# Fixing the engine order of the first batch, and the place of the weight conversions, in a three-stage attention, gated and spatial-gating kernel

## The chip, the cores and the metric

One core of one Trainium2 chip. The metric is device time in microseconds (us) of one execution; a kernel's time is the median of its runs. The kernel before took 771.68 us, the median of three runs (771.37 to 773.01).

## What is computed

Three blocks one after the other, for a batch of 8 sequences of 576 tokens with 512 channels, in fp32. The first two matter here:

```
kv  = einsum('bhsd,bhse->bhde', k, v)            # 8 heads of 64
o   = einsum('bhsd,bhde->bhse', q, kv)
x   = o / sqrt(mean(o*o, -1) + 1e-6) * g_norm    # heads joined: 512 channels

gate = sigmoid(causal 5-tap convolution of x along the tokens with conv_w)
y    = (gate * (x @ w_val)) @ w_out

...  # third block: y @ w_in, gelu, norm, a matmul over the tokens, @ w_out2, + y
```

The weights `w_val`, `conv_w`, `w_out`, `w_in` and `w_out2` reach the kernel as 64-bit floats, so each is read as pairs of 32-bit words and converted on the chip into a high part (fp32r, the format of the matmul) and a low part (the remainder). The products are formed as high*high + low*high + high*low.

## The kernel before, in words

**Tiling.** 512 channels are four groups m = 0 to 3 of 128. A batch has 512 main tokens (four tiles of 128) and 64 rest tokens (tile t = 4); the rest tokens of four batches are collected and multiplied together after batches 3 and 7. `x` is kept transposed: channels on partitions, tokens along the row. Every product with a weight (`gemm3`, L165, issued at L171) is 12 matmuls of 128 x 512.

**One batch.** `load_kv` and `load_q` (L192, L201) load; K, V and Q have one buffer each, so the next batch's load waits until the batch before has been read. `kv` (L205) forms the 64 x 64 products (80 matmuls, L220), `kv_out` copies them into a block-diagonal tile. `o(t)` (L234) gives one token tile (8 matmuls, L239) and queues three pieces: `norm` (square on ScalarE, sum on VectorE, scale and power -0.5 on GpSimd, L246 to L249), `scale` (VectorE, L252) and `transpose` (four on TensorE, L263; ScalarE copies into `x32`, L265, and into the high part, L268; VectorE forms the low part, L269). `conv(m)` (L283) is one ScalarE and four VectorE instructions (L285, L287) and a sigmoid. `Moe.val(m)` (L302) multiplies with `w_val` and queues `gated` (times the gate on VectorE, L312; high part on ScalarE; low part on GpSimd for m = 0 and 2, else on VectorE, L314). `Moe.out(m)` (L318) multiplies with `w_out`; all four m of the gated product have to be there first.

**Conversion of a weight** (`wide_parts`, L107, and `split`, L125). One piece is 128 columns of the weight, 128 x 512 elements on the chip for `w_val` and `w_out` (four pieces each, L560), 128 x 256 for `w_in` (16 pieces). A piece takes, in the form without GpSimd, an `Abs` on ScalarE (L113), L114 to L117 and L122 on VectorE, a copy on ScalarE (L151), a subtraction on GpSimd (L152) and an addition on VectorE (L153). With `on_pool` the product of L122 goes to ScalarE and GpSimd instead (L119, L120) and the addition to GpSimd. Half of the pieces of `w_val` and `w_out` have `on_pool` (L565). The raw words of `w_val` and `w_out` share one tile (`wiu` at that time), piece by piece; the pieces share two work areas (`wiv` at that time), so a third piece waits for the first. `w_in` later takes those two tiles over.

**What sets the order.** The program is written in slots: `later(n, fn, rank)` puts work n slots ahead, `tick` runs what is due. Beyond that the program is traced with a planner (L782) which, from a model of the time line, picks the order of instructions on each engine and may move an instruction ahead of others that stand before it in the program if its inputs are there. Each engine then runs its list strictly in order; SyncE's list holds every DMA issue. In the trace the conversion of `w_in`, which stands in the loop of batches 2 to 5 (L645 to L649), begins while batch 0 is still being prepared.

**The start before.** L565 to L611: the first two pieces of `w_val`, K and V, Q, the other two pieces and the small constants are loaded, two pieces are converted, then `kv` of batch 0, the `o` of batch 0 mixed with the loads of `w_out` and with `kv` of batch 1 (L592 to L600), then the other two pieces; the four `conv` and the four pieces of `w_out` are queued (L607 to L609), and the loop over the batches begins with `val` of batch 0 (L624).

Of the kernel before, what the change touches and what calls it, by code (L numbers as in the profile page):

```python
# [33 lines left out]
EXP_MAX = 1.875 * 2.0 ** -96  # L34

# [24 lines left out]
def body(ctx, tc, qT, k, v, gcol, w_val, conv_w, w_out, w_in, g_ln, w_sgT, b_sg, w_out2, out, out_r):  # L60
# [46 lines left out]
    def wide_parts(raw, t, on_pool):  # L107

        hi, lo = raw[:, :, 1], raw[:, :, 0]
        m, b, s = t[:, 0], t[:, 1].bitcast(I32), t[:, 2].bitcast(I32)
        act(m, hi.bitcast(F32), AF.Abs, scale=2.0 ** -112)  # L113
        ts(m, m, EXP_MAX, None, op0=ALU.min)  # L114
        ts(s, hi, -0x80000000, None, op0=ALU.bitwise_and)
        stt(b, m.bitcast(I32), 3, s, op0=ALU.logical_shift_left, op1=ALU.bitwise_or)
        ts(s, b, -0x800000, None, op0=ALU.bitwise_and)  # L117
# [5 lines left out]
        return f32(b), m  # L123

    def split(src, h, l, on_pool=False, raw=None, tmp=None, k=None):  # L125
# [8 lines left out]
        def start():  # L134
# [9 lines left out]
        def work():  # L144
# [5 lines left out]
            a, c = wide_parts(r.rearrange("p (n t) -> p n t", t=2), sb("cv", [3, n]) if tmp is None else tmp, on_pool)  # L150
# [4 lines left out]
        return start, work  # L155
# [25 lines left out]
    act(sb("st", [3, 8], bufs=3)[:, 0], mhalf, AF.Sigmoid)  # L181
# [5 lines left out]
    class Attention:  # L187
# [46 lines left out]
        def o(self, t, wait=3):  # L234
# [6 lines left out]
            st = sb("st", [3, 8], bufs=3)  # L241
# [3 lines left out]
            def norm():  # L245
                act(xo[:n], po[:n], AF.Square)  # L246
                nc.vector.tensor_reduce(st[:n, 0], x3, axis=AX.X, op=ALU.add)
                nc.gpsimd.tensor_scalar(st[:n, 1], st[:n, 0], 1.0 / DH, 1e-6, op0=ALU.mult, op1=ALU.add)
# [5 lines left out]

            later(0, norm, 0)
# [3 lines left out]
        def transpose(self, t, xo):  # L259
# [5 lines left out]
            act(x32[:, :, HALO + o:HALO + o + n], pt, AF.Identity, scale=gcol_s)  # L265
            if t < 4:
                xh, xl = self.xh[:, :, o:o + n], self.xl[:, :, o:o + n]
                act(xh, pt, AF.Identity, scale=gcol_s)  # L268
                stt(xl, pt, gcol_s, f32(xh), op0=ALU.mult, op1=ALU.subtract)  # L269
# [26 lines left out]
    class Moe:  # L296
# [5 lines left out]
        def val(self, m):  # L302
# [8 lines left out]
            def gated():  # L311
                tt(z, ps, self.g[:, m, :n], op=ALU.mult)  # L312
                act(zh, z, AF.Copy)
                (nc.gpsimd.tensor_tensor if m in (0, 2) else tt)(zl, z, f32(zh), op=ALU.subtract)  # L314

            later(0, gated, 0)

# [220 lines left out]

    def background(pieces, every, first=1, per=1):
# [20 lines left out]
    def first_weight(w, src, on_pool):  # L560
        return [split(src[:, m * P:(m + 1) * P], w[:, 0, :, m * P:(m + 1) * P], w[:, 1, :, m * P:(m + 1) * P],
                      on_pool[m], first[0][:, m], first[1][:, m % 2], k=NK)
                for m in range(NK)]

    wv_pieces, wo_pieces = first_weight(wv, w_val, (1, 0, 1, 0)), first_weight(wo, w_out, (0, 1, 1, 0))  # L565
    atts = [Attention(0)]
    wv_pieces[0][0]()
    wv_pieces[1][0]()
    atts[0].load_kv()
    atts[0].load_q()  # L570
    wv_pieces[2][0]()
    wv_pieces[3][0]()
    dma(gcol_s, gcol)
    dma(gln_s, g_ln)
    if conv_w.dtype == F32:
        dma(cw, conv_w)
    else:
        raw = sb("raw", [WC * 2], I32, bufs=2)[:, :2 * NK * KC]
        dma(raw, conv_w.bitcast(I32))
        a, c = wide_parts(raw.rearrange("p (n t) -> p n t", t=2), sb("cv", [3, NK * KC]), False)  # L580
        tt(cw, a, c, op=ALU.add)


    att = atts[0]
    wv_pieces[0][1]()
    wv_pieces[1][1]()
    att.kv(0)
    att.kv(1)
    tick()
    atts.append(Attention(1))  # L590
    atts[1].load_kv()
    for t in range(5):  # L592
        att.o(t, 2)
        tick()
        if t < 2:
            wo_pieces[t][0]()
        if t == 2:
            atts[1].kv(0)
            atts[1].kv(1)
            atts[1].load_q()  # L600
    tick()
    tick()
    wv_pieces[2][1]()
    wv_pieces[3][1]()
    wo_pieces[2][0]()
    wo_pieces[3][0]()
    for m in range(NK):  # L607
        later(m // 2, lambda m=m: att.conv(m), -1)
        later(m, wo_pieces[m][1], 3)  # L609
# [3 lines left out]
    for b in range(B):  # L613
        moe = Moe(atts[b].xh, atts[b].xl, gate, y_main[b])
# [8 lines left out]
        for s in range(8):  # L623
            if s < 4:  # L624
                moe.val(s)
            else:
                moe.out(s - 4)
            if b == 0 and s < 2:
                nxt.o(s)
# [15 lines left out]
            if b >= 2 and s % 2 and wi_n < len(wi):  # L645
                later(0, wi[wi_n][1], 3)
# [15 lines left out]
            tick()  # L662
        if b % RG == RG - 1:
# [124 lines left out]
```

## Time and profile before

| what | value |
|---|---|
| median of three runs | 771.68 us |
| the profiled execution | 771.06 us, of which the profile's span is 769.3 us |
| granted TensorE clock, mean over the span | 0.975 of 2.4 GHz |
| busy over the span: TensorE, VectorE, ScalarE, GpSimd | 94%, 77%, 46%, 23% |
| instructions | 11598 |

The profile has the busy time of each engine, the span in 40 slices, the chain of work that ended last, groups of instructions with what they waited for, and the DMA issues. A time line gives the start, the time taken and the count of like instructions that follow one another; the text in brackets is idle time of the engine in front of it and what ended it. PE is TensorE, DVE VectorE, ACT ScalarE, POOL GpSimd. A duration of a VectorE instruction overlaps the next one's by some 0.08 us when the two do not depend on each other.

### The profile page before, as it was taken

To read this page: it belongs to the slowest core of one execution; us is meant where nothing else is said; L and a number is where in the kernel's file an instruction comes from. 1 tells how busy PE (TensorE), PEld (TensorE's weight loads), DVE (VectorE), ACT (ScalarE), POOL (GpSimd) and SP (SyncE) were. 2 spreads that over 40 slices of the span, in tenths; PEclk is the share of its full clock that TensorE was granted. 3 is DMA by queue.
4 is the path that set the end of the run, shared out by engine and by line. 5 is a ranking of instruction groups with operands and counts; after the bars stand their busy time and mean duration, and the time that the engine had idled before them with its cause. 6 is when DMAs were issued, how large, how long until landed. Compare 5 with 4: busy or idle time off the path is not lost.

```text
span 769.3 us, 11598 instructions
## 1 busy us (share of the span) xinstructions
PE 724.7 (94%) x4400; PEld 621.9 (81%) x4400; DVE 590.2 (77%) x1118; ACT 350.0 (46%) x662; POOL 176.1 (23%) x186
## 2 busy tenths in 40 slices
PE   6529999999799999998999999999999999999997
PEld 6418778787787888887988988889899889898896
DVE  4979997988975968978977687776876867867662
ACT  3454755656535557456442343433432523434320
POOL 3763472635340725121000000010000000100000
PEclk8769999999999999999999999999999999999999
DMA  9852536355334310343212022121321221221203
GB/s 304 267 182 75 166 117 205 105 177 191 104 104 153 115 55 14 114 153 113 84 56 101 31 75 84 55 67 44 117 93 51 69 97 42 69 68 42 96 1 110
DMA packets 56199, 80.13 MB, mean 104 GB/s; under 512 B 3664, under 2 KB 29264, under 8 KB 55120
## 3 DMA queue, kind: packets, MB, share of 16 engines
q1 hardware_dynamic: 56144, 79.40, 31.1%
q8 instruction: 34, 0.56, 0.3%
q14 instruction: 21, 0.17, 0.1%
HBM read 60.51 MB, written 18.87 MB: 103 GB/s over the span
## 4 chain that ended last, share of the span: by engine, by line
PE 82%; DVE 7%; DMA 5%; ACT 3%; issue 1%; POOL 1%; SPq 0%; DVEq 0%; ACTq 0%
PE sg L507 15%; PE out L171 12%; PE val L171 12%; PE hu L171 11%; PE hv L398 11%; PE y L171 10%; PE o L239 4%; PE kv L220 3%; PE xT L263 2%; DVE G L287 2%; DMA wiu<-in_w_val_dram 2%; PE hur L171 2%; DMA raw<-y_main 1%; DMA K<-in_k_dram 1%; DMA raw<-in_w_out_dram 1%
## 5 line engine op out<-in xcount | busy, mean ns | idle before, releaser
L171 PE MATMUL y<-Z,WO 128*128 128x512 f32 (+1 forms) x480 | 111.5, 380 | 0.0
L287 DVE SCALAR_TENSOR_TENSOR G<-X,cw,G 128x576 f32<-128x576 f32 x128 | 101.2, 832 | 11.2 <-ACT G L285 11.2
L410 POOL TENSOR_TENSOR bmv<-bmv,mhalf 128x1 f32<-128x1 f32 x36 | 20.2, 560 | 346.0 <-DVE bmv L409 346.0
L171 PEld LDWEIGHTS y<-Z,WO 128*128 128x128 f32 x480 | 81.4, 188 | 15.5
L398 PE MATMUL hv<-wiv,X1h 128*128 128x512 f32 x256 | 83.3, 391 | 2.1 <-ACT X1h L375 2.0
L171 PE MATMUL out<-Z,X0h 128*128 128x512 f32 x256 | 82.9, 389 | 0.0
L171 PE MATMUL hu<-X1h,wiu 128*128 128x512 f32 x256 | 79.3, 391 | 0.0
L249 POOL TENSOR_TENSOR st<-st,mhalf 128x8 f32<-128x8 f32 (+1 forms) x40 | 73.1, 1828 | 2.8
L387 ACT ACTIVATE T<-T 128x512 f32<-128x512 f32 x68 | 42.9, 632 | 55.1 <-DVE T L384 55.1
L398 PEld LDWEIGHTS hv<-wiv,X1h 128*128 128x128 f32 x256 | 47.7, 188 | 12.0 <-ACT X1h L375 2.7
L171 PEld LDWEIGHTS out<-Z,X0h 128*128 128x128 f32 x256 | 48.1, 188 | 9.9
L171 PEld LDWEIGHTS hu<-X1h,wiu 128*128 128x128 f32 x256 | 46.5, 188 | 8.1
L508 DVE SCALAR_TENSOR_TENSOR T<-sg,gln,cv 128x288 f32<-128x288 f32 x64 | 32.8, 517 | 25.9 <-PE sg L507 25.8
L519 ACT ACTIVATE Z<-T 128x512 fp32r<-128x512 f32 x32 | 20.2, 633 | 66.9 <-DVE T L518 66.9
L263 PE MATMUL xT<-ident,T 128*128 128x128 f32 (+1 forms) x160 | 26.2, 286 | 26.0 <-DVE T L252 25.9
L171 PE MATMUL hu<-X1l,wiu 128*128 128x512 f32 x128 | 50.0, 391 | 0.0
L398 PE MATMUL hv<-wiv,X1l 128*128 128x512 f32 x128 | 49.9, 390 | 0.0
L171 PE MATMUL out<-Z,X0l 128*128 128x512 f32 x128 | 49.8, 389 | 0.0
L239 PEld LDWEIGHTS o<-kvbd,Q 128*128 128x128 f32 (+1 forms) x320 | 42.4, 192 | 5.9 <-issue 2.7
L239 PE MATMUL o<-kvbd,Q 128*128 128x128 f32 (+1 forms) x320 | 44.8, 288 | 0.6 <-DVE kvbd L232 0.6
L263 PEld LDWEIGHTS xT<-ident,T 128*128 128x128 f32 (+1 forms) x160 | 17.8, 148 | 33.1 <-issue 15.9
L171 PE MATMUL val<-X0h,WV 128*128 128x512 f32 x128 | 43.3, 420 | 0.0
(144 smaller groups left out, 1692.4 us busy)
## 6 DMA issues: line engine op xcount, KB each, us to landing
Q<-in_qT_dram SPq DMA_DIRECT2D x8, 1152.0 KB, 5.7
y_main<-Y SPq DMA_DIRECT2D x8, 1024.0 KB, 3.8
raw<-y_main SPq DMA_DIRECT2D x32, 256.0 KB, 3.2
Y<-y_main SPq DMA_DIRECT2D x32, 256.0 KB, 3.9
out_dram<-Y SPq DMA_DIRECT2D x32, 256.0 KB, 2.3
K<-in_k_dram SPq DMA_DIRECT2D x7, 1024.0 KB, 5.6
V<-in_v_dram SPq DMA_DIRECT2D x7, 1024.0 KB, 9.3
raw<-in_w_in_dram SPq DMA_DIRECT2D x16, 256.0 KB, 5.6
```

The costliest lines, as they stand in the source:

```text
L171: nc.tensor.matmul(ps, lhsT=a[:, kt, msl], rhs=x[:, kt], start=(i == 0), stop=(i == 3 * NK - 1))
L220: nc.tensor.matmul(self.pk[j][h, h], lhsT=self.k[:n, t, js][:, h], rhs=self.v[:n, t, js][:, h], start=(t == 0), stop=(t == 4))
L239: nc.tensor.matmul(po[:n, j * P:(j + 1) * P], lhsT=self.q[:, j, o:o + n], rhs=bd[:, j, :], start=True, stop=True)
L249: nc.gpsimd.tensor_tensor(st[:n, 2], st[:n, 1], mhalf[:n], op=ALU.pow)
L263: nc.tensor.transpose(pt[:, j * P:j * P + n], xo[:n, j * P:(j + 1) * P], ident[:n, :n])
L287: stt(g, x32[:, m, j:j + S], cw3[:, m, j:j + 1], g, op0=ALU.mult, op1=ALU.add)
L387: act(w, w, AF.Tanh, scale=CG * AG)
L398: nc.tensor.matmul(ps, lhsT=a[:, kt], rhs=p2["wiv"][:, w, kt], start=(i == 0), stop=(i == 3 * NK - 1))
L410: nc.gpsimd.tensor_tensor(mv[:, 3:4], mv[:, 2:3], mhalf[:, 0:1], op=ALU.pow)
L507: nc.tensor.matmul(ps, lhsT=a[:, msl], rhs=w, start=(n == 0), stop=(n == len(mm) - 1))
L508: later(0, lambda: stt(vs[:, sl], ps, gln_s[:, m:m + 1], p2["bsg"][:, sl], op0=ALU.mult, op1=ALU.add))
L519: act(g[:, 0], x, AF.Copy)
```

## The change

The first batch, from its loads to its gated products, is traced in a block (`tc.manual_schedule()`) in which the order written is the order on each engine. In it all four pieces of `w_val` are loaded first and converted first; the subtraction and the product run on VectorE, no piece of `w_val` or `w_out` uses GpSimd any more. The norm, the scaling and the low parts of the five token tiles follow in a written interleaving, then `val` and `conv` of batch 0, one piece of `w_out`, and `kv` of batch 1, which so moves behind `val`. The other three pieces of `w_out` and all pieces of `w_in` get an edge on each of the three elementwise engines (`issue_after`): they stay behind the block, or behind the slot three back. For batch 0 the small scaling of the norm and all low parts of the gated product are on VectorE. The `st` tile gets five buffers for three, and in `transpose` ScalarE writes the high part before `x32`.

```diff
-    def wide_parts(raw, t, on_pool):
+    def wide_parts(raw, t):
...
-        if on_pool:
-            act(m, lo.bitcast(U32), AF.Copy, scale=2.0 ** -52)
-            nc.gpsimd.tensor_tensor(m, m, f32(s), op=ALU.mult)
-        else:
+        def low():
+            ts(s, b, -0x800000, None, op0=ALU.bitwise_and)
             stt(m, lo.bitcast(U32), 2.0 ** -52, f32(s), op0=ALU.mult, op1=ALU.mult)
...
+        def rest():
...
+            a = st["steps"][1]()
             act(h, flat(a), AF.Copy)
-            nc.gpsimd.tensor_tensor(flat(a), flat(a), f32(h), op=ALU.subtract)
-            (nc.gpsimd if on_pool else nc.vector).tensor_tensor(l, flat(a), flat(c), op=ALU.add)
+            c = st["steps"][2]()
+            (nc.gpsimd.tensor_tensor if on_pool else tt)(flat(a), flat(a), f32(h), op=ALU.subtract)
+            tt(l, flat(a), flat(c), op=ALU.add)
...
+    def latest():
+        found = {}
+        for i in reversed(nc.cur_bb.bb.instructions):
+            if i.engine in ELEMENTWISE and i.engine not in found:
+                found[i.engine] = i
...
+        return list(found.values())
+
+    def behind(marks, fn):
+        with ExitStack() as pins:
+            for i in marks:
+                pins.enter_context(tc.issue_after(i))
+            fn()
...
+    with tc.manual_schedule():
+        for m in range(NK):
+            wv_pieces[m][0]()
+        att.load_kv()
+        dma(gcol_s, gcol)
+        dma(gln_s, g_ln)
+        cw_work = taps()
+        att.load_q()
+        atts[1].load_kv()
+        wv_pieces[0][2]()
+        for m in range(NK):
+            if m + 1 < NK:
+                wv_pieces[m + 1][2]()
+            wv_pieces[m][3]()
+            wo_pieces[m][0]()
+            if m < 2:
+                att.kv(m)
+            if m == 2:
+                cw_work()
+                slots.drain()
+        atts[1].load_q()
+        steps = [att.o(t, None) for t in range(5)]
+        lows = []
+        for t in range(8):
+            if t < 5:
+                steps[t][0](ts)
+            if 2 <= t < 7:
+                steps[t - 2][1]()
+                lows.append(steps[t - 2][2]())
+            if t >= 3:
+                lows[t - 3]()
+        moe = Moe(att.xh, att.xl, gate, y_main[0])
+        z = []
+        for m in range(NK):
+            z.append(moe.val(m, True))
+            att.conv(m)
+            if m:
+                z[m - 1][0]()
+            if m > 1:
+                z[m - 2][1](False)
+        wo_pieces[0][2]()
+        z[3][0]()
+        z[2][1](False)
+        wo_pieces[0][3]()
+        z[3][1](False)
+        atts[1].kv(0)
+        atts[1].kv(1)
+        slots.drain()
+    marks = [latest()]
...
+            if b == 0 and s < 3:
+                later(0, lambda s=s: behind(marks[0], wo_pieces[s + 1][1]), 3)
...
             if b >= 2 and s % 2 and wi_n < len(wi):
-                later(0, wi[wi_n][1], 3)
+                later(0, lambda w=wi[wi_n][1], m=marks[-3]: behind(m, w), 3)
...
             tick()
+            marks.append(latest())
```

Of a piece, function 0 loads, 2 is the `Abs` on ScalarE, 3 the rest, 1 both. `steps[t]` are norm, scale and transpose of a tile; `z[m]` are `gated` and its low part.

## Rows read from the trace of the kernel before

**Rows 1.** The page: busy time, and the granted clock in 40 slices of the span

```profile
PE 724.7 (94%) x4400; PEld 621.9 (81%) x4400; DVE 590.2 (77%) x1118; ACT 350.0 (46%) x662; POOL 176.1 (23%) x186
...
PEclk8769999999999999999999999999999999999999
```

**Rows 2.** Busy time by stretch: the start, then from one batch's first val on

```profile
core 0: us, PE busy (x) PEld busy (x) DVE busy (x) ACT busy (x) POOL busy (x), PEclk, DMA share, GB/s
0.00:55.50 55.50, 25.72 (x253) 22.79 (x253) 41.63 (x69) 23.03 (x44) 34.90 (x36) 0.75 0.80 261
55.50:94.70 39.20, 38.01 (x253) 31.07 (x253) 36.83 (x65) 25.25 (x49) 16.29 (x16) 0.92 0.36 112
94.70:128.90 34.20, 34.20 (x240) 27.27 (x238) 30.07 (x55) 20.08 (x39) 16.61 (x15) 1.00 0.46 158
128.90:162.80 33.90, 33.90 (x240) 27.19 (x238) 30.09 (x56) 22.07 (x42) 16.31 (x15) 1.00 0.47 160
...
196.90:218.90 22.00, 17.09 (x121) 16.38 (x120) 19.28 (x40) 10.40 (x24) 8.95 (x9) 0.92 0.20 75
...
249.40:283.40 34.00, 34.00 (x237) 27.17 (x237) 25.16 (x38) 19.11 (x35) 13.84 (x12) 1.00 0.19 67
```

**Rows 3.** Time line of TensorE in the first 56 us

```profile
13.58 2.96 PE L220 MATMUL kv<-V,K 128*64 128x64 f32 x48 [2.71 <-DMA V<-in_v_dram]
17.15 4.53 PE L239 MATMUL o<-kvbd,Q 128*128 128x128 f32 x24 [0.61 <-DVE kvbd L232]
...
54.91 0.66 PE L263 MATMUL xT<-ident,T 64*128 64x64 f32 x4 [7.31 <-DVE T L252]
```

**Rows 4.** The chain that ended last, 50 to 80 us: start, us, what

```profile
55.57 5.42 PE val L171 x12
...
67.65 2.80 PE val L171 x12
...
74.46 3.53 PE kv L220 x80
```

**Rows 5.** Busy time of the instructions on tile wiv (DVE, ACT, POOL), start

```profile
0.00:55.50 55.50, 0.00 (x0) 0.00 (x0) 30.12 (x40) 12.54 (x21) 22.75 (x16) 0.75 0.80 261
```

**Rows 6.** Time line of VectorE in the first 56 us

```profile
4.45 0.43 DVE L115 TENSOR_SCALAR wiv<-wiu 128x512 int32<-128x512 int32 x1 [4.45 <-DMA wiu<-in_w_val_dram]
...
7.36 1.74 DVE L116 SCALAR_TENSOR_TENSOR wiv<-wiv 128x512 int32<-128x512 int32 x1
...
30.60 0.69 DVE L153 TENSOR_TENSOR WV<-wiv 128x512 fp32r<-128x512 f32 x1
...
43.52 0.69 DVE L116 SCALAR_TENSOR_TENSOR wiv<-wiv 128x512 int32<-128x512 int32 x1
```

**Rows 7.** Time line of GpSimd in the first 56 us

```profile
7.29 1.27 POOL L120 TENSOR_TENSOR wiv<-wiv 128x512 f32<-128x512 f32 x1 [5.01 <-ACT wiv L119]
...
41.87 1.97 POOL L249 TENSOR_TENSOR st<-st,mhalf 128x8 f32<-128x8 f32 x1
```

**Rows 8.** Tile wiu: the product L122, duration in ns min/median/max

```profile
L122 DVE SCALAR_TENSOR_TENSOR wiv<-wiu,wiv x4: 691/1476/1753, 10.5 to 48.5; 128x512 f32<-128x512 uint32 x4
```

**Rows 9.** Busy time by stretch, the first 20 us (columns as Rows 2)

```profile
0.00:10.00 10.00, 6.30 (x41) 6.14 (x43) 5.16 (x8) 4.58 (x7) 4.42 (x12) 1.00 0.80 274
10.00:20.00 10.00, 6.68 (x91) 6.29 (x87) 4.85 (x10) 2.04 (x6) 3.15 (x3) 0.69 1.08 336
```

**Rows 10.** Groups in the first 56 us: the power -0.5 (busy us, mean ns)

```profile
L249 POOL TENSOR_TENSOR st<-st,mhalf 128x8 f32<-128x8 f32 (+1 forms) x5 | 9.1, 1825 | 0.2
```

**Rows 11.** Busy time of the instructions on tile cv (DVE, ACT, POOL), by stretch

```profile
55.50:94.70 39.20, 8.08 (x20) 3.23 (x8) 2.94 (x4) 0.92 0.36 112
94.70:128.90 34.20, 6.17 (x17) 2.11 (x5) 2.38 (x3) 1.00 0.46 158
128.90:162.80 33.90, 7.34 (x19) 3.03 (x7) 2.21 (x3) 1.00 0.47 160
...
196.90:218.90 22.00, 6.41 (x17) 2.12 (x5) 2.36 (x3) 0.92 0.20 75
```

**Rows 12.** Busy time of VectorE's convolution L287, from the first val on

```profile
55.50:94.70 39.20, 17.55 (x23) 0.92 0.36 112
```

More of the change, by code (lines that the diff above doesn't have):

```diff
@@ L132, in flat, with load @@
             return x.rearrange("p (k n) -> p k n", k=k) if k else x
-        def start():
+        def load():
             r = raw
@@ L142, in start, with first @@
             dma(flat(r), s.rearrange("(k p) n -> p k n", p=P) if k else s)
-        def work():
+        def first():
+            if wide:
+                st["steps"] = wide_parts(st["raw"].rearrange("p (n t) -> p n t", t=2),
+                                         sb("cv", [3, n]) if tmp is None else tmp)
+                st["steps"][0]()
+        def rest():
             r = st["raw"]
@@ L149, in work @@
                 return
[L150 removed]
+            a = st["steps"][1]()
             act(h, flat(a), AF.Copy)
[L152 to L155 removed]
+            c = st["steps"][2]()
+            (nc.gpsimd.tensor_tensor if on_pool else tt)(flat(a), flat(a), f32(h), op=ALU.subtract)
+            tt(l, flat(a), flat(c), op=ALU.add)
+        def work():
+            first()
+            rest()
+        return load, work, first, rest
     def split_weight(w, src, c0, n):
@@ L253, in scale @@
                    st[:n, 2].unsqueeze(2).to_broadcast([n, 8, DH]), op=ALU.mult)
+            if wait is None:
+                return norm, scale, lambda: self.transpose(t, xo, True)
             later(0, norm, 0)
@@ L268, in transpose, with low @@
                 act(xh, pt, AF.Identity, scale=gcol_s)
-                stt(xl, pt, gcol_s, f32(xh), op0=ALU.mult, op1=ALU.subtract)
+            act(x32[:, :, HALO + o:HALO + o + n], pt, AF.Identity, scale=gcol_s)
+            def low():
+                if t < 4:
+                    stt(xl, pt, gcol_s, f32(xh), op0=ALU.mult, op1=ALU.subtract)
+            if apart:
+                return low
+            low()
         def rest_parts(self):
@@ L300, in __init__, with val @@
             self.xh, self.xl, self.g, self.dst, self.n = xh, xl, g, dst, xh.shape[2]
-        def val(self, m):
+        def val(self, m, apart=False):
             n = self.n
@@ L313, in gated, with low @@
                 act(zh, z, AF.Copy)
-                (nc.gpsimd.tensor_tensor if m in (0, 2) else tt)(zl, z, f32(zh), op=ALU.subtract)
+            def low(on_pool=m in (0, 2)):
+                (nc.gpsimd.tensor_tensor if on_pool else tt)(zl, z, f32(zh), op=ALU.subtract)
+            if apart:
+                return gated, low
             later(0, gated, 0)
+            later(0, low, 0)
         def out(self, m):
@@ L566, in body, with taps @@
[L566 to L577, printed above, removed]
+    wv_pieces, wo_pieces = first_weight(wv, w_val), first_weight(wo, w_out)
+    att = Attention(0)
+    atts = [att, Attention(1)]
+    def taps():
+        if conv_w.dtype == F32:
+            dma(cw, conv_w)
+            return lambda: None
@@ L601, in body, with work @@
[L601 to L609, printed above, removed]
+        def work():
+            one, top, low = wide_parts(raw.rearrange("p (n t) -> p n t", t=2), sb("cv", [3, NK * KC]))
+            one()
+            a = top()
+            tt(cw, a, low(), op=ALU.add)
+        return work
+    with tc.manual_schedule():
[46 more added lines that the diff above has]
+        slots.drain()
```

61 lines of the change are left out of this document (24 added, 37 removed).

## The prediction, made before the changed kernel was built or run

> **What bounds the kernel now.** I read the page first, then the span by stretches, then the time lines of the first 56 us. TensorE is busy 94% of the span and only the first slices have a low granted clock [rows 1]. By stretches the picture splits at 55.5 us, the first `val` of batch 0: before it TensorE works 25.72 of 55.5 us, behind it 38.01 of 39.2, then all of 34.2 and all of 33.9 [rows 2]. So behind 55.5 us TensorE is the bound and a late start is lost for good. The gap in front is filled with VectorE's work, busy 41.63 us there, and the last wait in front of `val` is 7.31 us for the scaling of token tile 4 on VectorE [rows 2, 3]. What VectorE does there is mainly conversion: 30.12 us on VectorE and 22.75 us on GpSimd for eight pieces of `w_val` and `w_out` [rows 5], of which batch 0's `val` needs only the four of `w_val`.
>
> VectorE is also nearly full afterwards: 36.83 of 39.2 us beside batch 0, then about 30 of 34 per batch [rows 2]. That is what can take a gain back, since the change defers conversions.
>
> **When `val` starts after the change.** One piece on VectorE alone is seven instructions: L115, L114 and L117 at 0.43 us, L116 and L153 at 0.69 [rows 6], L122 at its unhindered 0.69 [rows 8], and the subtraction, which VectorE has never done here; its nearest row is L153, the same shape and two inputs, 0.69. Sum 4.05 us, four pieces 16.2. The stretched ones are gone: L116 took 1.74 us beside a GpSimd product of 1.27 [rows 6, 7], and eight pieces alone would be 32.4 us against the 30.12 plus GpSimd's 22.75.
>
> Step by step: the first piece lands at 4.45 us [rows 6]; the `Abs` adds about 0.7; three pieces end at 17.3. `conv_w` (six instructions of 20 columns) about 1.1: 18.4. Now `kv_out` stands in VectorE's list. K and V come behind 2.1 MB of `w_val`, 4.46 MB in all: 2.74 MB by 10 us at 274 GB/s, the rest at 336 GB/s by 15.1 [rows 9]; the last 48 `kv` matmuls 2.96 [rows 3] and the copies 0.8 give 18.9, so VectorE waits about 0.5 us. Piece 4 ends at 22.9. Q lands near 18.6, the five `o` take 1.51 us each at the low clock (24 matmuls, three tiles, in 4.53 [rows 3]) and stay ahead of VectorE. Sum of squares 0.7 and the small scaling 0.2 open the chain of powers at 23.8. Five powers of 1.825 us on one engine [rows 10], with 0.05 between them, last to 33.2; scaling 0.7, last low part 0.7, and TensorE's transposes beside them: `val` at about **35 us**, 20.5 us earlier. Bounds: 33 with the powers alone at 1.6, 39 if the K and V loads are 4 us later than the rates say.
>
> Do the powers on GpSimd hold VectorE up, as the product of 1.27 us did? L116, two inputs from on-chip memory, took its usual 0.69 us inside the 1.97 us power at 41.87 [rows 6, 7]: I take no cost. The Trainium skill, page "SBUF — State Buffer", section "Who interferes with whom", says otherwise: a GpSimd instruction that reads this memory shuts out a two-input VectorE instruction for its whole length. By that rule the sum would be the rival of the powers below, by the row it stays as it is; the trace disagrees with the rule for the power and agrees for the product.
>
> **What is put behind.** `kv` of batch 1 was done inside the old gap; now its 80 matmuls come behind `val`: +3.6 us of TensorE [rows 4]. The first `val` ran at the 1.2 GHz level, 5.42 us against 2.80 [rows 4], after an idle TensorE; it is idle in front of `val` again, so nothing changes.
>
> Batch 0's stretch then has 38.0 + 3.6 = 41.6 us of TensorE. VectorE had 36.83; minus `w_in` 8.08 [rows 11], now pinned to batches 2 to 5; minus 7 of 23 convolution steps, which belong to batch 1, 5.3 at 17.55/23 [rows 12]; plus four pieces of `w_out`, 16.2; plus two low parts from GpSimd, 1.4: 41.0 us. TensorE stays the bound by a hair, with no cover left. In the block VectorE's list is convolutions 12.2, eight gated and low instructions 5.5 and a piece 4.05, from 36.2: done at 58. TensorE has `val` 13.8 and `kv` 3.6 and the five `o` of batch 1 about 4.5: 57. Then `out(m)` waits for one piece each, some 4 us apart, while TensorE has 2.8 us of `out`, `kv` of batch 2, transposes. I take 2 us of gaps, between 0 and 12 (three pieces with nothing beside them). `val` of batch 1 then comes at 35 + 41.6 + 2 = 78.6 for 94.7.
>
> Batch 1's stretch loses the 6.17 us of `w_in` and gains the 5.3 of convolution: 29.2 of 34.2, free. Batches 2 to 5 carry four `w_in` pieces each, a piece being about 2.4 us (7.34/3 [rows 11]): batch 2 goes to 30.09 - 7.34 + 9.6 = 32.4 of 33.9, batch 5 to 25.16 + 9.6 = 34.8 of 34.0 [rows 2], 0.8 over. I add 1 us, between -5 and 17: below nothing, because the rest stretch at 196.9 has TensorE idle for 4.9 of 22 us [rows 2] while 6.41 us of `w_in` run on VectorE [rows 11], and most of those go.
>
> On SyncE the order moves too: batch 1's K and V wait there for batch 0's `kv` (about 18.5 us), and `w_out` and Q of batch 1 behind it. 2.4 + 2.1 + 1.2 MB at 336 GB/s land by about 36 us, first used near 49 us: nothing. K and V of batch 2 now wait for `kv` of batch 1 (about 53) and land near 62; used after that. The pins, the five `st` buffers and the swapped ScalarE copies cost no instruction; taken as 0, hidden under the power chain.
>
> **Sum**, against the profiled execution (771.06 us, a span of 769.3 and 1.76 around it): -20.5 + 3.6 + 2 + 1 = -13.9, so **757.1 us**. The median of the runs lies 0.6 above that execution, well inside the range.
>
> **Rivals.**
> - *VectorE becomes the bound beside batch 0.* For: 41.0 against 41.6 us leaves no cover, and its list is fixed until 58 us. If the norms of batch 1 (five times a sum, a scale and a low part, about 9.8 us) come behind all three remaining pieces (12.1), `val` of batch 1 starts at 58 + 12.1 + 9.8 + some 3 for the last power, transposes and copies = 83, plus 1 for a clock that falls in the gaps: gain 10.7 - 2 for batches 2 to 5: about **763**. Against: the planner may put the norms first.
> - *Slower.* The pinned `w_in`. Some 17 us of its work (8.08 + 6.17 and about 3 in the first 55) move from beside batches 0 and 1 into batches 2 to 5. If VectorE's idle 3.8 us per batch there [rows 2] is only waiting at a dependency and holds nothing, TensorE stands for all of it: 757 + 17 = **774**. It decides once a batch cannot take one more piece of 2.4 us. Against: those 3.8 us are one more than a piece, and before, three pieces per batch cost TensorE nothing.
> - *The powers stop VectorE* after all, as the product did: the five of batch 1, 9.1 us [rows 10], now fall beside two-input conversions on a VectorE without cover: 757 + 9 = **766**. Against: the 0.69 us row inside a power.
> - *The block does not hold its order*, and the planner lays out the start as before: **771**. Against: nothing in the trace can tell; the text of the change says it plainly.
> - *Faster.* The rest stretch's 4.9 us of idle go with the `w_in` pieces, and gaps stay at 0: **751**.
>
> **How the numbers follow.** Forecast 0.57, VectorE bound 0.20, powers 0.02, slower 0.07, no change 0.04, faster 0.10. Predicted is the forecast's 757. The range 750 to 766 holds the forecast, the faster case and the bulk of the VectorE case; outside are the slower case, no change, and about 0.06 of tails. About 0.2% of the time (1.5 us) is what a measurement of this kernel can tell from no change: faster 0.90, same 0.04, slower 0.06.
>
> **What would show it.** In the changed kernel's time line: `w_val` converted by about 23 us with no stretched VectorE instruction; five powers back to back until 33; the first `val` near 35; `kv` of batch 1 behind the fourth `val`; `val` of batch 1 near 79 with at most 3 us of TensorE idle between; the stretches of batches 2 to 5 as long as before. Wrong would be: `val` later than 39 (K and V late, or powers slower beside VectorE), TensorE waiting for WO on VectorE between 58 and 80, or stretches of batches 2 to 5 over 36 us.

## The result, and the profile after

The changed kernel takes 777.48 us (median of 7 runs, 775.57 to 779.78), the kernel before 772.09 (7 runs, 770.3 to 773.01): a ratio of 1.0076, 95% interval 1.0056 to 1.0096. It is slower by 0.8%; the forecast was 757 with a range of 750 to 766, and slower had 0.06. The profiled execution took 779.78 us with a span of 778.0.

The page after, busy time and granted clock in 40 slices (before: [rows 1]):

```profile
PE 729.2 (94%) x4400; PEld 625.5 (80%) x4400; DVE 593.6 (76%) x1141; ACT 348.5 (45%) x658; POOL 151.6 (19%) x163
...
PEclk8677999999899999999999999999999999999999
```

The sums hardly move, and they don't say where the time went. Five milestones of the two profiled executions do (starts from the time line of TensorE, us):

| kernel | first `val`, batch 0 | first `val`, batch 1 | first `val` of the second rest group | first `hu` | end |
|---|---|---|---|---|---|
| before | 55.5 | 94.7 | 323.9 | 363.3 | 769.3 |
| after | 42.8 | 97.4 | 326.4 | 370.6 | 778.0 |
| length, after minus before | -12.7 | +15.4 | -0.2 | +4.8 | +1.4 |

So there are two losses, not one. The start gives 12.7 us, and the stretch beside batch 0 takes 15.4. Batches 1 to 7 are as long as before. Then 4.8 us go at the change to the third block (`hv`, then `hur` and `hu`), with 1.4 behind it. Busy time by stretch of the changed kernel, with the same cuts (before: [rows 2]):

```profile
core 0: us, PE busy (x) PEld busy (x) DVE busy (x) ACT busy (x) POOL busy (x), PEclk, DMA share, GB/s
0.00:42.80 42.80, 22.55 (x173) 20.18 (x173) 27.09 (x57) 15.31 (x28) 9.88 (x15) 0.74 0.85 277
42.80:97.40 54.60, 43.60 (x333) 36.15 (x333) 47.04 (x76) 28.12 (x50) 11.35 (x10) 0.83 0.33 109
97.40:131.60 34.20, 34.20 (x240) 27.33 (x238) 25.05 (x38) 19.71 (x36) 13.83 (x12) 1.00 0.39 135
...
347.50:370.60 23.10, 17.35 (x105) 15.12 (x103) 20.09 (x43) 13.19 (x27) 4.46 (x6) 0.95 0.38 112
```

Beside batch 0 neither engine fills the 54.6 us: TensorE is idle for 11.0 and VectorE for 7.6. In batches 1 to 3 TensorE has no gap.

**The start.** TensorE's and VectorE's time lines, the last `kv` matmuls and the first step of `conv_w`:

```profile
17.78 3.02 PE L238 MATMUL kv<-V,K 128*64 128x64 f32 x48 [1.68 <-DMA V<-in_v_dram]
```

```profile
19.55 0.18 DVE L120 TENSOR_SCALAR cv<-raw 128x20 int32<-128x20 int32 x1 [2.95 <-DMA raw<-in_conv_w_dram]
```

V has landed at 17.8, not by 15.1, and VectorE, done with three pieces of `w_val` at 16.6, stands until `conv_w` is there. The six small steps of `conv_w` then end at 20.83 us, the `kv` matmuls at 20.80, so it was V that held up the copies behind both, and `conv_w` cost nothing beyond it.

**The stretch beside batch 0.** TensorE's time line there, then ScalarE's in front of the largest gap, then VectorE's in the block:

```profile
56.29 3.58 PE L238 MATMUL kv<-V,K 128*64 128x64 f32 x80
68.47 6.11 PE L257 MATMUL o<-kvbd,Q 128*128 128x128 f32 x39 [8.60 <-ACT kvbd L248]
```

```profile
65.24 0.61 ACT L340 ACTIVATE Z<-T 128x512 fp32r<-128x512 f32 x1
67.12 0.63 ACT L164 ACTIVATE WO<-wiv 128x512 fp32r<-128x512 f32 x1 [1.27 <-DVE wiv L122]
67.66 0.36 ACT L246 ACTIVATE kvbd<-kv 64x256 f32<-64x256 f32 x1
68.03 0.38 ACT L248 ACTIVATE kvbd<-kv 64x256 f32<-64x256 f32 x1
```

```profile
49.21 3.38 DVE L314 SCALAR_TENSOR_TENSOR G<-X,cw,G 128x576 f32<-128x576 f32 x4 [1.37 <-ACT G L312]
...
54.56 3.38 DVE L314 SCALAR_TENSOR_TENSOR G<-X,cw,G 128x576 f32<-128x576 f32 x4 [1.37 <-ACT G L312]
```

`kv` of batch 1 ends at 59.9, but the two copies that hand it on (0.36 and 0.38 us) stand in ScalarE's list behind the last gated copy and behind a copy of `w_out`, which itself waits 1.27 us for VectorE. TensorE waits 8.60 us for 0.74 us of work. In front of that VectorE waits 1.37 us for the second and for the third convolution and 0.76 for the fourth, because the ScalarE copy that opens a convolution (L312) stands behind the sigmoid that closes the one before.

The 8.60 us are not lost to ScalarE alone, though. While TensorE waits, and in the 12.6 us behind it, VectorE has hardly a gap (columns as above):

```profile
59.90:68.40 8.50, 0.00 (x0) 0.00 (x0) 8.28 (x14) 3.79 (x8) 0.00 (x0) 0.57 0.81 276
68.40:81.00 12.60, 10.21 (x124) 9.27 (x124) 12.57 (x25) 7.94 (x15) 7.50 (x8) 0.88 0.39 122
```

TensorE's next steps need that work too: the gated products and `w_out` for `y`, and then the norms and scalings of batch 1 for its transposes. TensorE's last wait ends at 81.07 us. Behind it the granted clock is 0.62 of full speed from 81.45 to 86.0, and the first `y` takes 4.58 us for the 3.06 before the change.

**The change of block.** VectorE's last instruction for the `w_in` pieces in tile `wiu`, after (before, the same group ran from 152.5 to 218.5), and TensorE's time line in front of `hur`:

```profile
L167 DVE TENSOR_TENSOR wiu<-cv x8: 406/423/524, 219.1 to 300.4; 128x256 fp32r<-128x256 f32 x8
```

```profile
368.72 2.08 PE L189 MATMUL hur<-WO,wiu 128*128 128x256 f32 x8 [4.11 <-ACT WO L513]
```

The same place before, TensorE:

```profile
362.25 1.22 PE L171 MATMUL hur<-WO,wiu 128*128 128x256 f32 x8 [0.89 <-ACT WO L481]
```

`w_in` is converted 82 us later, with nothing lost beside the batches; but what queues behind it, the conversion of `w_out2`, has its last VectorE instruction at 361.3 for 357.5 (2.5 of these 3.8 us are the whole program being later by then, 326.4 for 323.9). `hur` waits 4.11 us for 0.89 and then runs its eight matmuls in 2.08 for 1.22 us, at a granted clock of 0.50 (1.2 GHz) for 1.00 (2.4 GHz).

### The profile page after: what moved, and what is told of

Its sections match the earlier page's. It is cut to its first block, busy times and chain, and to the rows that moved or that the text cites. A ratio compares the mean times of both kernels' runs of the same rounds, so it can differ in the third digit from the quotient of the medians.

```text
span 778.0 us, 11571 instructions
## 1 busy us (share of the span) xinstructions
PE 729.2 (94%) x4400; PEld 625.5 (80%) x4400; DVE 593.6 (76%) x1141; ACT 348.5 (45%) x658; POOL 151.6 (19%) x163
## 4 chain that ended last, share of the span: by engine, by line
PE 78%; DVE 10%; DMA 7%; ACT 2%; issue 1%; SPq 0%; DVEq 0%; ACTq 0%
PE sg L539 15%; PE out L189 12%; PE hu L189 11%; PE hv L430 11%; PE y L189 9%; PE val L189 8%; DVE G L314 4%; PE o L257 4%; PE xT L283 3%; PE kv L238 2%; PE hur L189 2%; DMA V<-in_v_dram 1%; DMA raw<-y_main 1%; DMA raw<-in_w_in_dram 1%; DMA raw<-y_rest 1%
## 5 line engine op out<-in xcount | busy, mean ns | idle before, releaser
L419 ACT ACTIVATE T<-T 128x512 f32<-128x512 f32 x68 | 42.9, 631 | 48.5 <-DVE T L416 48.4
L257 PEld LDWEIGHTS o<-kvbd,Q 128*128 128x128 f32 (+1 forms) x320 | 43.1, 196 | 14.7 <-ACT kvbd L248 8.7
L539 PE MATMUL sg<-WV,V 128*128 128x288 f32 x192 | 43.4, 296 | 0.0
L539 PE MATMUL sg<-WV,K 128*128 128x288 f32 x192 | 43.0, 296 | 0.0
```

The source lines that it names most:

```text
L257: nc.tensor.matmul(po[:n, j * P:(j + 1) * P], lhsT=self.q[:, j, o:o + n], rhs=bd[:, j, :], start=True, stop=True)
L419: act(w, w, AF.Tanh, scale=CG * AG)
L539: nc.tensor.matmul(ps, lhsT=a[:, msl], rhs=w, start=(n == 0), stop=(n == len(mm) - 1))
```

## The experiments

The theory was: the loss beside batch 0 is order on ScalarE's and VectorE's lists, and the loss at the change of block comes from the pins on `w_in`. The main rival was VectorE as the bound beside batch 0 whatever the order. All ratios are to the kernel before, with 95% intervals. The milestones of all kernels stand in one table at the end of this section.

**1. `kv` of batch 1 one convolution earlier.** On the changed kernel, in the block:

```diff
             z.append(moe.val(m, True))
+            if m == NK - 1:
+                atts[1].kv(0)
+                atts[1].kv(1)
+                slots.drain()
             att.conv(m)
...
-        atts[1].kv(0)
-        atts[1].kv(1)
-        slots.drain()
```

> The changed kernel with kv of batch 1 and its copies written in front of the fourth convolution instead of at the end of the block; TensorE's order stays val, kv, o. Theory (the wait of 8.6 us for those copies is ScalarE's list order): the o of batch 1 begin near 61 for 68.5 us, the wait falls below 2 us, val of batch 1 comes near 91 for 97.4, and the time falls by 5 to 8 us, to about 771. Rival (VectorE, with the deferred w_out, is the bound beside batch 0): the wait only moves to the first y, val of batch 1 stays within 2 us of 97.4, and the time within 2 us of the changed kernel's 777.5.

Measured: 789.19 us, ratio 1.0215 (1.0183 to 1.0246): slower still. The wait for `kvbd` fell from 8.6 to 0.9 us, as the theory had it, and `val` of batch 1 came at 100.6. The waits of TensorE, 30 to 375 us:

```profile
PE y L189 <- ACT WO L164: 6.4, 3, 5.2
...
PE kv L238 <- DMA V<-in_v_dram: 3.8, 2, 3.3
PE y L189 <- DVE WO L167: 2.3, 1, 2.3
```

Behind the block the planner now put convolution steps of batch 1 ahead of the last piece of `w_out`, and `y` waited for that piece. The stretch of batch 1 is longer too, 38.3 us for 34.2, since 11 of batch 0's 48 matmuls of `y` now fall behind that mark. Both theories had the time too low; the rival was right that the wait only moves on to `y`, but it forecast no change. One wait removed alone was handed to the next one.

**2. The norms in front of the scalings.** On the changed kernel: the five `norm` first, then scaling and transposes tile by tile.

```diff
-        for t in range(8):
-            if t < 5:
-                steps[t][0](ts)
-            if 2 <= t < 7:
-                steps[t - 2][1]()
-                lows.append(steps[t - 2][2]())
-            if t >= 3:
-                lows[t - 3]()
+        for t in range(5):
+            steps[t][0](ts)
+        for t in range(6):
+            if t < 5:
+                steps[t][1]()
+                lows.append(steps[t][2]())
+            if t:
+                lows[t - 1]()
```

> The changed kernel with the five norms of batch 0 written in front of the first scaling, so that no square on ScalarE stands behind the copies of an earlier token tile. Theory (late val is the order of ScalarE's list): five powers back to back from 26.5 us on, the first val near 37 for 42.8, everything behind it 4 to 6 us earlier, time about 772. Rival (VectorE is the bound behind val): val near 37, but val of batch 1 within 2 us of 97.4, time within 2 us of 777.5. A second rival (the loads of K, V and Q bound the start): val not before 41.

Measured: 775.17 us, ratio 1.0040 (1.0024 to 1.0057). GpSimd's powers in the changed kernel, then in this one:

```profile
26.50 4.89 POOL L267 TENSOR_TENSOR st<-st,mhalf 128x8 f32<-128x8 f32 x3 [24.22 <-DVE st L266]
33.12 1.64 POOL L267 TENSOR_TENSOR st<-st,mhalf 128x8 f32<-128x8 f32 x1 [1.73 <-DVE st L266]
37.68 1.63 POOL L267 TENSOR_TENSOR st<-st,mhalf 64x8 f32<-64x8 f32 x1 [2.92 <-DVE st L266]
```

```profile
24.98 8.09 POOL L267 TENSOR_TENSOR st<-st,mhalf 128x8 f32<-128x8 f32 x5 [22.70 <-DVE st L266]
```

In the written order ScalarE has the squares of tiles 3 and 4 behind the copies of tiles 0 and 1, and those wait for TensorE's transposes, so the last two powers start late. With the norms first the five run back to back. The first `val` comes at 37.1, 20.9 us behind the last `kv` matmuls for 25.0. That is 4.1 us of the start; in the median 2.3 us of them are left.

**3. and 4. The pins on `w_in`.** Once taken away from the changed kernel, once put alone on the kernel before:

```diff
-                later(0, lambda w=wi[wi_n][1], m=marks[-3]: behind(m, w), 3)
+                later(0, wi[wi_n][1], 3)
```

> The changed kernel without the edges on w_in's conversion. Theory (the edges keep w_in going until 300 us, so that the pieces of w_out2 and the loads of y_rest come late at the change of phase, some 5 us): w_in is converted by about 220 us again, the first hu is late against the kernel before by no more than val of batch 1 is, and the time is 3 to 6 us under the changed kernel's, 772 to 774. Rival (w_in would crowd VectorE beside batch 0, which the edges prevent): val of batch 1 later by 4 us or more, time 777 or more.

> The kernel before with the edges on w_in's conversion as the one part of the change. Theory (the edges cost at the change of phase): batches 0 and 1 not slower than before, w_in until about 300 us, 3 to 6 us lost between 285 us and the first hu, time 775 to 778. Rival (the edges are harmless or help, since VectorE is freed beside batch 0): 769 to 772.

Measured: without the pins 773.71 us, ratio 1.0021 (1.0008 to 1.0033); the pins alone on the kernel before 777.89 us, ratio 1.0073 (1.0058 to 1.0088). TensorE in front of `hur`, without and with:

```profile
361.87 1.21 PE L189 MATMUL hur<-WO,wiu 128*128 128x256 f32 x8 [1.00 <-ACT WO L513]
```

```profile
366.15 2.08 PE L172 MATMUL hur<-WO,wiu 128*128 128x256 f32 x8 [3.73 <-ACT WO L482]
```

The pins alone cost as much as the whole change (5.8 us; taken off the changed kernel they give 3.8 back), and the rest of the change together comes out 1.6 us above the kernel before, with its `val` 14.7 us earlier. In the kernel before with pins, `val` of batches 1 to 3 came at 94.7, 128.7 and 162.8, as in [rows 2]: nothing of the price is paid beside the batches.

**5. Both at once.** Edits 2 and 3 on the changed kernel.

> The changed kernel with both earlier edits at once: the five sums and scalings of the norm in front of the first scaling, and the w_in pieces without their pins. Theory (two separate causes whose gains add): first val near 36, val of batch 1 near 88, first out of the pair stage below 395, 769 to 772 us. Rival (VectorE beside batch 0 or the planner's order takes the earlier start back): val of batch 1 at 92 or later, 773 us or more.

Measured: 769.90 us, ratio 0.9975 (0.9965 to 0.9986). The time is the theory's, but `val` of batch 1 came at 92.9, where the rival had it, and not at 88: of the earlier start some was eaten again beside batch 0, where the wait for `kvbd` is still 8.59 us.

**6. The copies that open the convolutions.** On kernel 5, with `conv` cut in two:

```diff
             z.append(moe.val(m, True))
-            att.conv(m)
+            if m + 1 < NK:
+                conv_copy(m + 1)
+            conv_rest(m)
```

> As the run before, and in the block ScalarE's copy that opens the convolution of tile m+1 stands in front of the sigmoid of tile m. Theory (the three idles of 1.37 us on VectorE in the block come from ScalarE's list alone): they go, the block's last VectorE instruction comes some 4 us earlier, 766 to 768 us. Rival (VectorE then waits for TensorE's val in the same place, or is full behind the block anyway): val of batch 1 as in the run before, time within 1 us of it.

Measured: 764.59 us, ratio 0.9918 (0.9893 to 0.9943). The idle times of 1.37 are gone from VectorE's list, `val` of batch 1 comes at 87.0 and the stretch beside batch 0 falls from 54.7 to 49.3 us. An order of ScalarE's list, with not one instruction less, was worth 5.3 us of the time, more than the theory's 766 to 768.

**7. All of `w_out` in the block.** On kernel 6: `kv` and its copies before the last convolution, the four pieces of `w_out` written in the block, the convolutions of batch 1 pinned behind it.

```diff
-        wo_pieces[0][3]()
-        z[3][1](False)
-        atts[1].kv(0)
-        atts[1].kv(1)
-        slots.drain()
+        for m in range(NK):
+            if m + 1 < NK:
+                wo_pieces[m + 1][2]()
+            wo_pieces[m][3]()
+            if m == 0:
+                z[3][1](False)
...
-                    later(1, lambda a=nxt, m=s - 4: a.conv(m), 2)
+                    later(1, lambda a=nxt, m=s - 4: behind(marks[0] if a.b == 1 else [], lambda: a.conv(m)), 2)
```

> As the run before, and kv of batch 1 with its copies stands before the last convolution of batch 0, all four w_out pieces are written in the block, and batch 1's convolutions are pinned behind the block. Theory (what is left beside batch 0 is order: kvbd late on ScalarE's list, w_out behind batch 1's convolutions): TensorE's wait for kvbd below 2 us, val of batch 1 near 85, 760 to 764 us. Rival (VectorE's time for w_out and the norms of batch 1 is the bound beside batch 0, whatever the order): VectorE over 95% busy from 45 us to the val of batch 1, which is no earlier than in the run before; time within 2 us of it.

Measured: 768.83 us, ratio 0.9958 (0.9940 to 0.9976): worse than kernel 6, and neither theory's. The wait for `kvbd` was 0.9 us, but TensorE then waited 4.2 us for V of batch 2, whose load had become the next late thing, and batch 1 took 37.4 us (89.6 to 127.0) for 34.7, with the convolutions deferred into it. VectorE was not full (21.75 of 28 us from 62 to 90). Of the loss 1.6 us are a first `val` at 39.3 for 37.7, so already the start. Which of the three edits cost the gain was not tried apart.

**8. Less work for VectorE.** The changed kernel without the low half's conversion in three pieces of `w_out`. A ScalarE copy writes the value itself where the remainder belongs, so the kernel leaves out more than the precision that the expectation names: its product is not the right one, and it serves for its time only.

```diff
+            if short:
+                act(l, flat(a), AF.Copy)
+                return
             c = st["steps"][2]()
```

> The changed kernel without the low half's conversion in the last three pieces of w_out (two conversions, the subtraction and the addition on VectorE, some 2.2 us each; a ScalarE copy writes the low half in their place), so it leaves out part of the weight's precision. Theory (VectorE's time beside batch 0 decides when val of batch 1 starts): val of batch 1 near 91 for 97.4, 771 to 773 us. Rival (TensorE's wait for the kvbd copies on ScalarE decides): val of batch 1 within 2 us of 97.4, 776 to 778 us.

Measured: 774.59 us, ratio 1.0034 (1.0022 to 1.0045). Twelve VectorE instructions are gone and three ScalarE copies are added; VectorE's busy time in the stretch is 40.92 us for 47.04, 6.1 less. `val` of batch 1 came at 90.9, as VectorE's theory had it, and the time lies between the two theories. But 3 us of that is a first `val` at 39.8 (below); the stretch is 51.1 us for 53.1 to 54.6 in the four kernels with this start and full work, and the wait for `kvbd` was 8.2. So VectorE's work counts, at 2.0 to 3.5 us of the 6.1.

**9. The copies of `kv` on kernel 6.** The three lines of `kv` and its copies stand in front of `w_out`'s first piece and the last gated product.

```diff
+        atts[1].kv(0)
+        atts[1].kv(1)
+        slots.drain()
         wo_pieces[0][2]()
         z[3][0]()
         z[2][1](False)
         wo_pieces[0][3]()
         z[3][1](False)
-        atts[1].kv(0)
-        atts[1].kv(1)
-        slots.drain()
```

> As the run with the convolution's copies moved (764.59 us), and batch 1's kv with its copies stands in every engine's list in front of the last gated product and of w_out's first piece, instead of behind both. Theory (VectorE, busy without a break from 39 to 75 us there, decides when val of batch 1 starts): TensorE's wait for the kvbd copies falls from 5.3 to below 1.5 us, val of batch 1 comes at most 1.5 us earlier than 87.0, 763 to 765 us. Rival (TensorE's wait is lost time): val of batch 1 near 83, 760 to 761 us.

Measured: 762.95 us, ratio 0.9882 (0.9867 to 0.9897), the fastest kernel of the study. TensorE's time line in kernel 6 and in this one:

```profile
59.59 7.40 PE L257 MATMUL o<-kvbd,Q 128*128 128x128 f32 x39 [5.30 <-ACT kvbd L248]
```

```profile
56.88 6.48 PE L257 MATMUL o<-kvbd,Q 128*128 128x128 f32 x40 [1.39 <-ACT kvbd L248]
```

`val` of batch 1 came at 83.2: here the rival was right about the place, and the theory, for which VectorE left no room, about the time (762.95 for 763 to 765). The windows show how both can be:

```profile
37.90:83.20 45.30, 40.63 (x323) 33.59 (x322) 42.93 (x70) 27.29 (x50) 10.35 (x10) 0.90 0.42 142
83.20:118.90 35.70, 35.70 (x251) 29.20 (x249) 34.22 (x59) 22.01 (x43) 18.41 (x16) 1.00 0.46 152
```

The stretch beside batch 0 falls by 4.0 us, with VectorE busy 42.93 of 45.3 (in kernel 6 46.01 of 49.3), and batch 1 takes 1.0 us more with VectorE busy 34.22 of 35.7 (32.57 of 34.7): work of VectorE moved across the mark, and by the medians 1.6 us of the 4 are left in the time. The two intervals overlap, but each of this kernel's four runs lies below each of kernel 6's.

**10. `conv_w`, K and V before the last piece of `w_val`.** On kernel 6:

```diff
-        for m in range(NK):
+        for m in range(NK - 1):
             wv_pieces[m][0]()
+        cw_work = taps()
         att.load_kv()
         dma(gcol_s, gcol)
         dma(gln_s, g_ln)
-        cw_work = taps()
+        wv_pieces[3][0]()
         att.load_q()
```

> As the run with the convolution's copies moved (764.59 us), and in SyncE's list conv_w and K and V stand in front of the fourth piece of w_val. Theory (the start waits for K and V, so first val keeps its 21.4 us behind the last kv matmuls): conv_w no longer waited for, the last kv matmuls 1 to 1.7 us earlier than 16.3, first val near 36.3, 763 to 763.5 us. Rival (VectorE's four pieces set the start): fourth piece's end at 24.7 and first val at 37.7 unchanged, time within 0.5 us of 764.6.

Measured: 767.43 us, ratio 0.9936 (0.9920 to 0.9953), a miss of both. The last `kv` matmuls were earlier (15.3 for 16.3), but VectorE and TensorE show what was late instead:

```profile
18.80 0.69 DVE L166 TENSOR_TENSOR wiv<-wiv,WV 128x512 f32<-128x512 f32 x1 [2.78 <-ACT WV L164]
```

```profile
21.54 7.75 PE L257 MATMUL o<-kvbd,Q 128*128 128x128 f32 x40 [3.19 <-DVE kvbd L250]
```

The fourth piece landed late, ScalarE stood at its `Abs` in front of its copy for the third, VectorE waited 2.78 us for that copy, and its copies for `kvbd` came behind. The first `val` was at 39.6 for 37.7.

**11. and 12. What `w_out2`'s lateness holds up.** On the changed kernel with its pins. First only other buffers for the first two loads of `y_rest`; then these loads also moved in front of the loads of `w_sgT` and `b_sg`, a slot earlier:

```diff
-            raw = [sb("raw", [NK, P], bufs=2) for c in range(RW // P)]
+            if g:
+                raw = [sb("raw", [NK, P], bufs=2) for c in range(RW // P)]
+            else:
+                raw = [tmp(NK * P).rearrange("p (k n) -> p k n", k=NK) for c in range(RW // P)]
```

```diff
                     if s == 4:
+                        y_r = Group.load(0)
                         sg_weight(stage)
...
-                    if s == 5:
-                        y_r = Group.load(0)
```

> The changed kernel with its pins, but the first two loads of y_rest for the pair stage go to buffers of their own (tile T) and no longer share the two raw buffers with w_out2's pieces. Theory (at the phase change the pinned w_in makes w_out2 late, and these loads wait for its buffers): TensorE's wait in front of hur falls from 4.1 to below 1.5 us, 773 to 775 us. Rival (ScalarE and VectorE are late themselves there): a wait of 3 us or more stays in front of hur or of the next tiles, 777 us or more.

> As the run with the rest loads in buffers of their own (778.34 us), and SyncE's list has these two loads in front of the loads of w_sgT and b_sg. Theory (SyncE's list is in order: b_sg's load waits for the one cv buffer until the last piece of w_out2 leaves it, and the y_rest loads stood behind b_sg): they are issued 3 us or more earlier than 361.7, TensorE's wait in front of hur falls from 5.65 to below 2 us, 773 to 775.5 us. Rival (what is late there is ScalarE's and VectorE's work itself): hur starts within 1.5 us of 369.2, or the next wait takes over, 777 us or more.

Measured: 778.34 us, ratio 1.0074 (1.0053 to 1.0095), and 775.20 us, ratio 1.0051 (1.0035 to 1.0066). SyncE's time line in the changed kernel, in run 11 and in run 12:

```profile
360.26 0.52 SPq L520 DMA_DIRECT2D raw<-y_rest  x1
360.87 1.22 SPq L371 DMA_DIRECT2D T<-in_w_sgT_dram  x2
362.14 0.58 SPq L761 DMA_DIRECT2D cv<-in_b_sg_dram  x1
362.76 0.56 SPq L520 DMA_DIRECT2D raw<-y_rest  x1
```

```profile
361.11 0.58 SPq L764 DMA_DIRECT2D cv<-in_b_sg_dram  x1
361.73 1.23 SPq L523 DMA_DIRECT2D T<-y_rest  x2
```

```profile
358.06 1.25 SPq L523 DMA_DIRECT2D T<-y_rest  x2
359.37 1.26 SPq L371 DMA_DIRECT2D T<-in_w_sgT_dram  x2
360.73 0.53 SPq L765 DMA_DIRECT2D cv<-in_b_sg_dram  x1
```

My first reading, the shared `raw` buffers alone, fell with run 11: in buffers of their own both loads still went out at 361.73, and the wait for `hur` grew to 5.65 us. The load of `b_sg` is into the one `cv` buffer, which the last piece of `w_out2` leaves at 361.8 (VectorE's L167 at 361.33 in the changed kernel), and in SyncE's list both loads of `y_rest` stood behind it in run 11, the second of them in the changed kernel. In the kernel before both stood in front of it (355.85, `b_sg` at 358.22). In run 12 they go out 3.7 us earlier than in run 11, 1.8 of which are the whole program being earlier there, and the wait falls to 1.66 us. By the medians that gives 2.3 of the 3.8 us by which run 3 lies below the changed kernel, but the intervals overlap. From the second rest `val` to the first `hu`, which leaves the scatter of the start out, it gives 3.0 of 5.5 us: 44.2 in the changed kernel, 41.2 in run 12, 38.7 in run 3. What is left, small waits of `hv` among it, was not tried one by one.

The milestones of all kernels (us, profiled executions; medians of the runs in the last column; a profiled execution lies up to 3.1 us from its median, run 2's 772.07 below, run 11's 781.16 above):

| kernel | first `val` | `val`, batch 1 | second rest `val` | first `hu` | end of span | median |
|---|---|---|---|---|---|---|
| 1 `kv` earlier | 41.6 | 100.6 | 334.7 | 379.3 | 787.2 | 789.19 |
| 2 norms first | 37.1 | 90.2 | 319.2 | 362.5 | 770.3 | 775.17 |
| 3 no pins | 40.8 | 94.0 | 324.2 | 362.9 | 769.6 | 773.71 |
| 4 before + pins | 56.3 | 94.7 | 324.1 | 368.0 | 776.2 | 777.89 |
| 5 = 2 + 3 | 38.2 | 92.9 | 322.4 | 361.1 | 768.3 | 769.90 |
| 6 = 5 + copies | 37.7 | 87.0 | 317.2 | 356.0 | 762.8 | 764.59 |
| 7 = 6 + `w_out` | 39.3 | 89.6 | 322.9 | 361.7 | 768.6 | 768.83 |
| 8 less VectorE | 39.8 | 90.9 | 320.4 | 363.6 | 771.6 | 774.59 |
| 9 = 6 + `kv` copies | 37.9 | 83.2 | 315.6 | 353.7 | 760.7 | 762.95 |
| 10 = 6 + load order | 39.6 | 89.0 | 319.7 | 358.5 | 765.9 | 767.43 |
| 11 loads apart | 41.4 | 96.0 | 325.3 | 371.1 | 779.4 | 778.34 |
| 12 loads first | 41.2 | 94.3 | 323.5 | 364.7 | 771.9 | 775.20 |

From the second rest `val` to the first `hu` the kernels without pins, the kernel before among them, take 38.1 to 39.4 us, those with pins 43.2 to 45.8, and run 12 takes 41.2. From there to the end all kernels take 406.0 to 408.3.

## Why the prediction was wrong

- **The start** (20.5 us earlier): 12.7, so 7.8 short. Two steps were too short. K and V were there at 17.8 us for the 15.1 worked out from [rows 9], 2.7 us; `conv_w`, behind them, came late too, but was done when they were. And "five powers back to back" did not hold: the written order gave them the gaps of run 2, 4.1 us. The pieces themselves took 3.92 us each for 4.05, with no stretched instruction.
- **The powers beside VectorE** (no cost): right, but the row given for it is misread. L116 at 43.52 starts 0.32 us before that power ends at 43.84, so it does not lie inside it. A row that does is in the same trace: L116 at 22.16, 0.69 us, inside the power from 21.51 to 23.30. After the change the same shows in batch 1 (last section). In run 2 the five powers took 8.09 us, 1.62 each against the 1.825 of [rows 10].
- **The stretch beside batch 0** (41.6 us and 2 of gaps): this is the step that failed; it took 54.6. TensorE was idle for 11.0 us where 2 were taken, and its own work took 43.6, 2.0 more, at the lower clock behind the gap (1.5 of them in the first `y`). The sum for VectorE, 41.0 for a measured 47.04, took off seven convolution steps of batch 1, but the planner ran eight of them there all the same (24 for 23 [rows 12]). That was not what cost the time: the eight begin at 91.55 us, behind TensorE's last wait. What cost it is what I did not look for: I asked of each engine how much work it had, and of TensorE and VectorE in which order, but never read ScalarE's list, 28 us full of 54.6, on which both the convolutions and `kvbd` wait. So VectorE stood still for 3.5 us in the block and was full from 59.9 to 81 us, and TensorE's steps behind it came late. Order alone, in runs 6 and 9, takes the stretch from 54.7 to 45.3; what is left over the 43.6 of the forecast goes with a VectorE busy for 42.9.
- **The sum.** For this stretch it adds 3.6 + 2 = 5.6 us, but its own lengths, 43.6 for 39.2, make 4.4: the 1.2 us that TensorE was idle there before are counted twice. That is small beside the miss.
- **The rival "VectorE becomes the bound"** (763, 0.20) was about the right place, and in part about the mechanism: VectorE was full behind the block. It had neither the 3.5 us that VectorE stood still in front of that nor the size. VectorE's work and the order both count: run 8 took 6.1 us of work from it and the stretch got 2.0 to 3.5 shorter, run 6 took none and it got 5.4 shorter.
- **The pins on `w_in`** (+1): 5.8 us, run 4 against the kernel before, and 3.8 in the changed kernel, run 3. Beside batches 2 to 5, where forecast and slower rival both had looked, they cost nothing, so the rival's 774 came near the time for a wrong reason. The step counted VectorE's time only. It missed what stands behind `w_in`: the same tiles `cv` and `raw` and SyncE's list carry on to `w_out2` and to the first loads of the third block. The rest stretch's idle time did not go either: TensorE worked 17.39 of 22.3 us there.
- **`kv` of batch 1** (+3.6): 3.58 at the higher clock. The swapped copies and the buffers were not tried apart.

The forecast's idea, that `w_val` first gives an earlier `val`, was right, and with the order mended and the pins off it is worth 1.2% (run 9). Written as it was, its gain was eaten in the very next stretch, and the pins' price was left.

## What to carry to other kernels

When an order is written out by hand, go through the list of every engine, the lightly loaded one too: here ScalarE, busy half of the stretch, held up two fuller engines because short copies stood behind instructions that themselves waited. When work is deferred, follow its buffers and its DMA queue to whoever takes them over, up to the next change of stage; where the work itself runs may be free. And remove waits in the order in which they end: one taken away alone (run 1) made the kernel slower, since the planner filled the room with something else.

## What the runs showed of the hardware

**Landing times.** The same first loads land at different times from run to run. The last `kv` matmuls, which wait for V, began at 17.78 in the changed kernel, 16.47 in run 1, 15.53 in run 3, 14.91 in run 8, 16.07 in run 11 and 16.89 in run 12, all with the same loads, and the first `val` followed 24.3 to 25.3 us behind. So a start that waits for loads passes their scatter on. The kernels with it spread wider between runs (4.2 us for the changed kernel, 4.9 for run 3, where the kernel before has 2.7 in 7 runs and 3.1 in 23); that the loads are the cause of that was not tried.

**GpSimd shut out.** In run 1 a scaling of 128 x 8 elements on GpSimd, 0.19 to 0.90 us in the changed kernel, took 4.89 while VectorE went through two-input instructions, and one of one input (L121, 0.41 us), with hardly a break. GpSimd, then VectorE:

```profile
87.62 4.89 POOL L266 TENSOR_SCALAR st<-st 128x8 f32<-128x8 f32 x1 [7.92 <-DVE st L265]
```

```profile
87.46 0.67 DVE L167 TENSOR_TENSOR WO<-wiv 128x512 fp32r<-128x512 f32 x1
88.06 2.99 DVE L314 SCALAR_TENSOR_TENSOR G<-X,cw,G 128x576 f32<-128x576 f32 x4
90.98 0.41 DVE L307 TENSOR_TENSOR XR<-X,XR 128x256 fp32r<-128x256 f32 x1
91.31 0.41 DVE L121 TENSOR_SCALAR wiv<-wiv 128x512 f32<-128x512 f32 x1
91.65 0.80 DVE L314 SCALAR_TENSOR_TENSOR G<-X,cw,G 128x576 f32<-128x576 f32 x1
```

It ends with the last of them, at 92.5. The power behind it comes late by that, and VectorE then waits 1.81 us for the power, at 94.26. Before, GpSimd's long product stretched VectorE [rows 6, 7]; here the small one is held off by VectorE. The Trainium skill, page "SBUF — State Buffer", section "Who interferes with whom", says that a VectorE instruction with two inputs from this on-chip memory and a GpSimd instruction that reads it contend for a lock, and that the order of issue decides who is blocked. The trace agrees for this scaling, if it loses to each following instruction in turn. It does not agree for the power: in batch 1 of the changed kernel one takes its usual 1.64 us while a two-input conversion step inside it takes its usual 0.68 (GpSimd, then VectorE):

```profile
75.95 1.64 POOL L267 TENSOR_TENSOR st<-st,mhalf 128x8 f32<-128x8 f32 x1
```

```profile
76.33 0.68 DVE L127 SCALAR_TENSOR_TENSOR wiv<-wiu,wiv 128x512 f32<-128x512 uint32 x1
```

Another power, at 80.47, did take 2.55 us. The scalings beside the powers of run 2 say nothing on this, since one of their inputs comes from the memory that the matmul writes.
